# Cross-shaped window attention on one core: all matmuls in 64x64 tiles, VectorE's exponential as three shifted terms, and a written-out order

## The chip, the cores and the metric

The kernel runs on 1 core of a Trainium2 chip. The metric is the device time of one launch in microseconds. The kernel before takes 1006.58 us (median of 3 runs, 1004.67 to 1014.27).

## The reference

Input x is one image of 224 x 224 tokens with 96 channels in bf16. The channels are split in two halves of 48: the first half attends inside horizontal stripes of 8 rows, the second inside vertical stripes of 8 columns. There are 28 windows of each kind, and each has 1792 tokens.

```
qkv = einsum('bhwc,cd->bhwd', x, wqkv);  q, k, v = thirds of qkv
qh, kh, vh = first 48 channels, reshaped to (28, 8*224, 48)          # horizontal stripes
ah = softmax(qh @ kh^T * 48**-0.5);  oh = ah @ vh
qv, kv, vv = last 48 channels, transposed and reshaped to (28, 224*8, 48)   # vertical stripes
av = softmax(qv @ kv^T * 48**-0.5);  ov = av @ vv
out = concat(oh, ov) @ wo
```

The bulk is 56 windows of 1792 x 1792 scores, their exponentials, and the product of the exponentials with V.

## The kernel before, in words

Two windows are worked on together as a pair P (28 pairs: 14 horizontal, then 14 vertical), called w = 0 and w = 1; w = 0 lives on partitions 0 to 63, w = 1 on 64 to 127. The queries of a pair come in four chunks c of 512, 512, 512 and 256 (`CH`). The keys come in 14 tiles of 128. A *unit* is one key tile of a 512-chunk, or two key tiles of the 256-chunk, for both windows: 49 units per pair, 1372 in all.

For each unit TensorE computes the scores of both windows (`qk_op`, L1016: K^T of 48 rows x 128 keys against 512 queries) into two neighbouring PSUM banks. K is centred and scaled beforehand, Q carries the factor, and a unit's scores come out as 128 times the base-2 exponent. Then the unit's exponential is made in one of two ways:

- *ScalarE's units* (`add_a`, 1071 of them): one activation Exp over both banks into a tile PT (L1038). Then the values product (`pv_op`, L969: V of 128 keys x 64 columns against PT), one matmul per window into two column halves of the chunk's accumulator bank. A column of ones in V gives the sum of the exponentials.
- *VectorE's units* (`add_d`, 301 of them, `NDC` and `NDP` say how many per chunk, mostly two units together): VectorE adds an offset and converts to int16 (L1076, I_sb), whose bits read as bf16 are a rough power of two. Two mask steps (L1089, U_sb; L1091, E_sb) and a product I*U (L1095, G_sb; mostly on GpSimd in pieces of 512, else on VectorE) make a two-term correction: the values product is done twice, once with E and once with G.

When a chunk is complete VectorE evacuates the accumulator (L932, OT_sb); `fin` projects it with wo (L810, L844), takes the reciprocal of the sums (L797) and multiplies (L817, L854). Horizontal results are kept in Ph_sb; for vertical pairs GpSimd adds them (L860) and SyncE stores (L888, 16 stores per pair). Beside this `prep(P + 1)` projects K (L706), Q (L700) and V (L766) of the next pair with `fill` matmuls over all 96 channels (L686, L761); GpSimd centres K (L720). `load(P + 2)` brings x transposed, by DMA transposes on SyncE's queue (L558): one per horizontal window and eight per vertical one, into xT_sb, which has two buffers.

The order of all engines comes out of a `Planner` that runs when the kernel is built: per engine an order string (`PLAN["pe"]` and so on) names the stream that the next operation is taken from, a "bank" string the PSUM banks, and a "far" string which products go to GpSimd. Each engine's instructions then run strictly in that order, with semaphore waits for what they depend on. The chip's PSUM has eight banks; scores take two per unit, accumulators and fills one each.

The planner also keeps VectorE's fast SBUF-to-SBUF steps and GpSimd's operations apart (`lock`): a GpSimd operation waits for the last such VectorE step ahead of it.

Of the kernel before, what the change touches and what calls it, by code (L numbers as in the profile page):

```python
# [11 lines left out]
ALU = mybir.AluOpType  # L12

E_MID = 1.513  # L20
ONE = 127.0 - log2(E_MID)
M_FRAC, M_EXP, HALF, E_LOW = 0x007F, 0x7F80, 0x3F00, 0x0002


NDC = [4, 2, 2, 2]
NDP = {P: [3, 3, 3, 2] for P in range(28) if P % 4 != 1}


def ndc(P, c):
    return NDP.get(P, NDC)[c]  # L30


PLAN = {
    "pe": (
        "0000000000000000000000066611216162164144116444216331216431241641231431643441163446141541234133164412164412144312314"
        "31631451431244144126143153121433146124153341143444131235144123414414126413311463643164154134143163124614412614"
        "31145444134124163135164123135412144414412433112344144116344416312351431241641134445312416411463344144121543123"
        "14611364451231441163441233154113444412614412416312513411433444146123153114634413351541241634124136144123144116"
        "34434134124136134125144412316411463441213341146354154164144123133412314412414412316341163444135123164135414124"
        "41441461231634124133113644413312541441231641146344124313411634312441341261441231341441233144114644512316433153"  # L40
        "12416412314313411644431154444416415431531361241544123164114634114453341541231641241634125144144124133114434412"
        "54144113336412461441164431245143126134114533441414612351331241641146343124414411363412531441134464126134125144"
        "12413313412341541441163533416124415312461341144431163444412134412416313361441241541241631146441132331544113444"
        "12641441261331231341145444415412316311463433125144123164114534412341641146334144125413413312416441241641136441"
        "12444133113644312416441215431341241344123144164133123161331146345124153411444412361341134444615415416431313512"
        "44164123164114344412316311453441264134125144144124313312514414414611363354131254144123413416412416411463343141"
        "45124416313412416341241461113443344125144412133316412164412415411433334154124146134126133411634412441544121633"
        "11433544144164123154123146311446341241441164333125144113644512314314412441441612313412361341153444126133411263"
        "41441153444123416411463431333124154124163411264414411534441163354123164145123134412144414613312414312316441231"
        "44146135135312414414412613331163441144464451441331631241534124164114634114433441251344114644126314412514414123"  # L50
        "13412315411344436131641253144124163413514412416411463334143123146124134114644441214461133344125143411442154136"
        "12316412313313414412415441136446133125413124415411364441231544114634413313316441261341241641231441641144334125"
        "41341441231341241541241641146333134415413124414126133123154113644412315441146334154164144412613312316312464144"
        "11644341241334114634124415412415313613412413314364411444412531213314412313414313441241541163344143123154123154"
        "41146346114644611444463134151244415412316412416314412416411333441251344141153344412513341441241341241543164133"
        "14416412316312461441146443123144116336415312415314124413416412416412416412313313415441146341253134123154114464"
        "31244136144115343341431631241631241644126134114644412413311464441231334151244154124164124133113464431152344131"
        "34125134414412313415411463344154164164123163312416313464144126144144123153312414414412315312416411463331344164"
        "31441246144125144313412414414414615312361331231541136444412415411464441133644311344431531241531241641231641146"
        "44412413314441251334141125313341123444136144125144411463331463134125144412416411444334121641163363151244154124"  # L60
        "16312414316412164411433431231541144434415123315441231541144344123416411463341441246144121633113343412416441116"
        "36336124154124153124164134146124133124134134144415412415311633631541264431441254144134114334413441261331446121"
        "63414441231441126413311463441241541241531231614612431431331444144125143123314414412315441115336346113444641541"
        "64146163313613412414412614411344441231534124154124164114644412313412133411464441133633124415412315411344431251"
        "44411433441541241421316311366334166144164123134124144124154123153411466441313412441441231334154124153114444451"
        "312351331144444123313411434412541331241544113444124314311443152334154114421433114431433151534414445"),
    "dve": (
        "00000000000000000333333332332344323232443233313443432323244123443234323321342444133234423233333344133232333414"
        "23334323442322144313233244333233441323323333244312344323232344431323343133332342432344143232332344123443333332"
        "42421234413332344342333232144323323443214442323442424133321333244233344333331333233234431333323234243324124331"  # L70
        "32344323323344133323323444231323443323233244412334333132332443332144323233234431234432323244431333234312332344"
        "33233314423323234432144323423432412443123333244332344333333313323234412333234432321443233133323443232333413342"
        "32324431423443232324443134332312344323323344331323323443231233344234423321234431323234434323344132332323443313"
        "33234423442332124423133334423233443333132332344312333234421233244331332334432332334413232443231234432333234442"
        "41233431323323344323344413332323244314234423233234441344423132323344323344333313232323443214432332333444423144"
        "21244442343233441323323333334431333233234423231442313334234423233441343232334442133333423443232323444123343123"
        "32334443234441333323232344321444323323323214434441323234443233443331333234233442312344232332344344132314234442"
        "33332332334132334344441333233232344321444213323444323233443132332344432133333233244323234441233441332332344432"
        "34413232344432313332332334423324444412332313333323442344413423332444213234432332332334444421214423323333344333"
        "33333132234412332332344421234443132332344323441334232343333343242123323344334424412332313443432334442414423323"  # L80
        "34442144332343424444143333133333"),
    "pool": (
        "00000000022222221212122222222222222222112122222222222222221212122222222222222222221112222222222222222222211122"
        "22222222222222222121212222222222222222221212122222222222222222212112222222222222222222221212122222222222222222"
        "21212122222222222222222221112222222222222222222121212222222222222222222121212222222222222222222212121222222222"
        "22222222212121222222223223222232222121213222233332222322222121212222233322332232222333112122222222233223322331"
        "21213222232222332222121213222222333223222221211322222222333322222213131322223332222322222233321212123223222233"
        "2222222121212332232222223333221311222222332222222222212121232233332232222222222313112233322223333322333333"),
    "far": (
        "11111011110111111101111111111111111011111111110111011111111111111111101111111111111111111111111101111111111111"  # L90
        "11110111111111111111110111111111111111111111111110111011101100111111110010010111111010101101111001110111010111"
        "011110101100110110110111101101110111011100101101111111101011111011010100001000000"),
    "bank": (
# [23 lines left out]
class Op:  # L117
    __slots__ = ("eng", "occ", "lat", "fn", "deps", "soft", "alloc", "then", "wait", "tok", "dma", "mode", "start", "end", "lock", "segs", "kind", "far", "late")

    def __init__(s, eng, occ, lat, fn, deps=(), soft=(), alloc=(), then=None, dma=None, mode=None):  # L120
# [3 lines left out]
        s.kind, s.far, s.late = None, (), None  # L124


class Pool:


    def __init__(s, slots):  # L130
        s.slots = list(slots)
        s.free_by = {k: [] for k in s.slots}
# [1092 lines left out]
```

## Time and profile before

| what | value |
|---|---|
| median of 3 runs (range) | 1006.58 us (1004.67 to 1014.27) |
| profiled execution, span from first to last instruction | 1001.1 us (the page gives no other time of it) |
| PE (TensorE matmul) busy | 987.2 us, 99% |
| ACT (ScalarE) busy | 987.6 us, 99% |
| DVE (VectorE) busy | 938.3 us, 94% |
| POOL (GpSimd) busy | 684.3 us, 68% |
| granted TensorE clock | 0.998 |

How to read it: a busy PE is modelled, since matmuls are pipelined and overlap. In the rows of groups stand the line, the engine, the operation, output<-input with shapes and the count, then busy us and the mean ns of one, then the idle time of the engine just before and what ended it. In a timeline the first two numbers are start and length. PEld is the loading of weights for a matmul. The windows view gives, for each stretch, busy time and count on PE, PEld, DVE, ACT and POOL, the granted clock, and the DMA's share and GB/s.

### The profile page before, as it was taken

The numbers are of one execution on the slowest core, as the hardware profiler recorded it, in microseconds if no ns is written. First come the engines' busy times: TensorE is split into PE (matmuls) and PEld (weight loads), VectorE is DVE, ScalarE is ACT, GpSimd is POOL, SyncE is SP. The second block draws the span as 40 slices with busy tenths as digits, with TensorE's granted clock in tenths as the row PEclk, the third lists the DMA queues.
The fourth block names the chain that finished last, engine by engine and source line by source line (L and its number), as shares of the span: only waits on it lengthen the run. The fifth ranks groups of instructions, "written<-read, shape, count | busy, mean of one in ns | idle before, by whom it ended". The sixth has DMA issues, their size and how long they took to land.

```text
span 1001.1 us, 24570 instructions
## 1 busy us (share of the span) xinstructions
PE 987.2 (99%) x10216; PEld 385.3 (38%) x10216; DVE 938.3 (94%) x1573; ACT 987.6 (99%) x1080; POOL 684.3 (68%) x660
## 2 busy tenths in 40 slices
PE   8999999999999999999999999999999999999997
PEld 3333433343343334334334333433433443343342
DVE  8989999999999999999899999999999999999997
ACT  7999999999999999999999999999999999999997
POOL 3677776667677676777776776776676777677652
PEclk9999999999999999999999999999999999999999
DMA  5101110210222023011111122222122222222012
GB/s 110 39 7 33 38 38 2 38 39 1 38 39 32 7 38 38 2 37 24 26 30 32 26 46 49 54 50 46 36 40 53 52 52 41 52 52 37 16 34 52
DMA packets 164712, 36.92 MB, mean 37 GB/s; under 512 B 164488, under 2 KB 164488, under 8 KB 164600
## 3 DMA queue, kind: packets, MB, share of 16 engines
q1 hardware_dynamic: 163016, 34.80, 18.4%
q8 instruction: 80, 1.31, 0.5%
q10 hardware_dynamic: 1584, 0.55, 0.2%
q14 instruction: 32, 0.26, 0.1%
HBM read 0.44 MB, written 9.63 MB: 10 GB/s over the span
## 4 chain that ended last, share of the span: by engine, by line
ACT 70%; PE 28%; DVE 1%; DMA 0%; issue 0%
ACT PT L1038 70%; PE ps L969 13%; PE ps L1016 11%; PE ps L686 2%; PE ps L761 1%; PE ps L844 1%; DMA w_sb<-in_wqkv_dram 0%; PE ps L810 0%; DVE OT_sb L932 0%; DVE out_sb L867 0%; DVE I_sb L1076 0%; DVE U_sb L1089 0%; DVE E_sb L1091 0%; PE ps L679 0%; DVE KT_sb L706 0%
## 5 line engine op out<-in xcount | busy, mean ns | idle before, releaser
L1038 ACT ACTIVATE PT<-ps 128x1024 bf16<-128x1024 f32 x1071 | 983.5, 1114 | 2.9 <-PE ps L1016 1.5
L1095 POOL TENSOR_TENSOR G_sb<-I_sb,U_sb 128x512 bf16<-128x512 bf16 x482 | 544.1, 1153 | 250.0 <-DVE E_sb L1091 224.6
L1016 PE MATMUL ps<-QT_sb,KT_sb 48*128 48x512 bf16 (+1 forms) x3136 | 463.0, 356 | 4.7 <-ACT PT L1038 3.0
L1076 DVE TENSOR_SCALAR I_sb<-ps 128x1024 int16<-128x1024 f32 x301 | 367.4, 1220 | 24.7 <-PE ps L1016 21.3
L969 PE MATMUL ps<-PT,V_sb 128*64 128x512 bf16 (+1 forms) x2422 | 363.8, 363 | 1.1 <-ACT PT L1038 1.0
L1016 PEld LDWEIGHTS ps<-QT_sb,KT_sb 48*128 48x128 bf16 x3136 | 123.2, 93 | 307.4 <-ACT PT L1038 223.3
L969 PEld LDWEIGHTS ps<-PT,V_sb 128*64 128x64 bf16 x2422 | 119.2, 109 | 122.6 <-issue 94.9
L969 PE MATMUL ps<-G_sb,V_sb 128*64 128x512 bf16 (+1 forms) x714 | 115.7, 356 | 0.0
L969 PE MATMUL ps<-E_sb,V_sb 128*64 128x512 bf16 (+1 forms) x714 | 109.9, 356 | 0.5 <-DVE OT_sb L932 0.2
L1089 DVE TENSOR_SCALAR U_sb<-I_sb 128x2048 int16<-128x2048 int16 (+1 forms) x161 | 109.1, 678 | 0.2
L860 POOL TENSOR_TENSOR out_sb<-tmp,Ph_sb 128x480 bf16<-128x480 f32 (+1 forms) x84 | 84.9, 1025 | 30.0 <-DVE E_sb L1091 10.7
L1091 DVE TENSOR_SCALAR E_sb<-I_sb 128x2048 int16<-128x2048 int16 (+1 forms) x161 | 104.9, 652 | 0.2 <-PE ps L969 0.2
L686 PE MATMUL ps<-xT_sb,w_sb 96*64 96x512 bf16 (+1 forms) x444 | 77.5, 366 | 1.0 <-ACT PT L1038 0.5
L932 DVE CAST OT_sb<-ps 128x512 bf16<-128x512 f32 x112 | 69.3, 619 | 5.9 <-PE ps L969 5.0
L706 DVE TENSOR_SCALAR_CACHE_REDUCE KT_sb<-ps 128x512 bf16<-128x512 f32 x110 | 67.8, 620 | 7.4 <-PE ps L686 6.8
L700 DVE TENSOR_SCALAR QT_sb<-ps 128x512 bf16<-128x512 f32 (+1 forms) x111 | 68.1, 619 | 5.3 <-PE ps L686 4.1
L766 DVE CAST V_sb<-ps 128x480 bf16<-128x480 f32 (+2 forms) x85 | 51.7, 612 | 3.1 <-PE ps L761 2.8
L969 PEld LDWEIGHTS ps<-G_sb,V_sb 128*64 128x64 bf16 x714 | 36.4, 108 | 47.3 <-issue 28.8
L720 POOL TENSOR_SCALAR KT_sb<-KT_sb,negmean 128x1792 bf16<-128x1792 bf16 x27 | 47.5, 1759 | 10.3 <-DVE E_sb L1091 6.2
L817 DVE TENSOR_TENSOR Ph_sb<-ps,rc 128x480 bf16<-128x480 f32 (+1 forms) x84 | 52.3, 622 | 2.1
L854 DVE TENSOR_TENSOR tmp<-ps,rc 128x480 f32<-128x480 f32 (+1 forms) x84 | 51.9, 618 | 2.2
L969 PEld LDWEIGHTS ps<-E_sb,V_sb 128*64 128x64 bf16 x714 | 33.9, 108 | 42.9 <-issue 21.3
(49 smaller groups left out, 323.0 us busy)
## 6 DMA issues: line engine op xcount, KB each, us to landing
out_dram<-out_sb SPq DMA_DIRECT2D x208, 42.0 KB, 2.1
xT_sb<-in_x_dram SPq DMA_TRANSPOSE x251, 2.4
out_dram<-out_sb SPq DMA_DIRECT2D x22, 24.0 KB, 1.9
Ph_sb<-in_x_dram ACTq DMA_DIRECT2D x1, 336.0 KB, 3.1
out_dram<-out_sb ACTq DMA_DIRECT2D x6, 24.0 KB, 1.9
wo_sb<-in_wo_dram SPq DMA_DIRECT2D x4, 9.0 KB
wo_sb<-one_sb SPq DMA_DIRECT2D x4, 0.0 KB
w_sb<-in_wqkv_dram ACTq DMA_DIRECT2D x1, 54.0 KB, 4.7
```

Of the source, the lines that this page charges most:

```text
L686: ins = e.matmul(bk[64 * w:64 * w + 64, 0:qs], lhsT=w_sb[0:C, wblk(P, kind), :], rhs=rhs, start=True, stop=True)
L700: return e.tensor_scalar(dst, src, QS, None, ALU.mult)
L706: return e.tensor_scalar(dst, src, 1.0, None, ALU.mult, ALU.add, accum_out=acc)
L860: return e.tensor_tensor(out_sb[b][:, k0:k0 + nk, ws[0], :], t, Ph_sb[:, k0:k0 + nk, j0 + ws[0], :], ALU.add)
L932: return e.tensor_copy(OT_sb[b][:, q0:q0 + qs], bk[:, 0:qs])
L969: return e.matmul(bank(k.bank)[64 * w:64 * w + 64, x0:x1], lhsT=lhs(w, kts[i])[p0:p1], rhs=rhs(w, i, qs)[p0:p1, x0:x1], start=(op.tok["fir ...
L1016: ins = e.matmul(bank(op.tok["s"][w])[:, i * qs:(i + 1) * qs], lhsT=KT_sb[b][64 * w:64 * w + C2, kt * 128:(kt + 1) * 128], rhs=QT_sb[b][64 ...
L1038: a.fn = lambda e: e.activation(PT[a.tok["p"]][:].rearrange("p (s n) -> p s n", s=2), two(q.tok["s"]), ACTF.Exp, scale=LN128)
L1076: return e.tensor_scalar(dst[:, at:at + 1024].rearrange("p (s n) -> p s n", s=2), two(src), 128.0 * ONE, 0.0, ALU.add, ALU.max)
L1089: f.fn = lambda e: e.tensor_scalar(U_sb[y()][:, 0:m], I_sb[y()][:, 0:m], M_FRAC, HALF, ALU.bitwise_and, ALU.bitwise_or)
L1091: x2.fn = lambda e: e.tensor_scalar(E_sb[x2.tok["l"]][:, 0:m], I_sb[y()][:, 0:m], M_EXP, E_LOW, ALU.bitwise_and, ALU.bitwise_or)
L1095: g.fn = lambda e: e.tensor_tensor(G_sb[x2.tok["l"]][:, i0:i1], I_sb[y()][:, i0:i1].bitcast(BF16), U_sb[y()][:, i0:i1].bitcast(BF16), ALU. ...
```

## The change

- *Tiles.* Every matmul of the steady state uses 64x64 tiles of the array. Scores of window w go from row half w to column half w, in two half-units of 64 keys (`qk`); each half-unit's two windows share one bank, on different partition halves. Values go from row half w to column half 1 - w (`pv`), with 64 keys at a time and V of 50 columns. K, Q and V projections are done in two halves of 48 channels on the scores' tiles; the output projection uses 49 rows. PE has four semaphores instead of one, by tiles used.
- *Layout of x.* So that half the channels of both windows stand on the two partition halves, window 0 is transposed into xa_sb and window 1 into a staging tile xr_sb; three SBUF-to-SBUF copies per pair (SyncE's queue) place the rest. wqkv is loaded a second time in halves (w2_sb).
- *VectorE's units.* 13 per pair instead of 10 or 11 (`ND`), so 364; ScalarE has 1008. For 11 of the 13, the exponential is the sum of three bf16 readings: of I, of I + 43 and of I + 85, with V scaled by 2^(-43/128) and 2^(-85/128) for the last two (Vs_sb, made by GpSimd once per pair). The adds are int16 steps over one or two units, 272 on GpSimd and 64 on VectorE; the values product is done three times. Two units per pair keep the old masks and product.
- *Order.* The planner is gone. One string `SEQ` (10743 letters) gives the order of everything, and `BANK` the banks; each engine runs its own operations in that order.

The core of the diff (the old strings and the planner's classes, which go, are left out):

```diff
-NDC = [4, 2, 2, 2]
-NDP = {P: [3, 3, 3, 2] for P in range(28) if P % 4 != 1}
+T_MID = 3.122
+ONE3 = 127.0 - log2(T_MID)
+SHIFT = (43, 85)
+ND = ["4432"]
+QUAD = [(5,)]
...
+    S, M = 0.2165, 0.0315
...
 def load(P, stream):
...
+                dst_, sem_ = (xr_sb, s_xr) if w else (xa_sb[b], s_x[b])
...
+                if not w:
+                    hi = wk.add(stream, Op("sp", 0.65, lambda e: e.dma_start(xb_sb[b][0:C2, 0, :], xa_sb[b][C2:C, 0, :]), [op] + war, ...))
+            for src, dst in ((0, xa_sb), (C2, xb_sb)):
+                last = wk.add(stream, Op("sp", 0.65, lambda e, src=src, dst=dst: e.dma_start(dst[b][64:64 + C2, 0, :], xr_sb[src:src + C2, 0, :]), [op, hi], ...))
...
 K and Q projections:
+                    for i in range(1 if startup else 2):
+                        for w in range(2):
+                                src, wt = (xa_sb, xb_sb)[i][b][64 * w:64 * w + C2, 0, :], w2_sb[i][64 * w:64 * w + C2, wblk(P, kind), :]
+                            ins = e.matmul(out_, lhsT=wt, rhs=rhs, start=i == 0, stop=startup or i == 1)
...
+        def qk(u, stream):
+            for h, t in enumerate(ts):
+                th = [2 * kts[0] + h] if len(kts) == 1 else [2 * kts[h], 2 * kts[h] + 1]
+                def fn(e, t=t, th=th):
+                    for i, k in enumerate(th):
+                        for w in range(2):
+                            ins = e.matmul(bank(t.k)[64 * w:64 * w + 64, i * qs:(i + 1) * qs], lhsT=KT_sb[b][64 * w:64 * w + C2, 64 * k:64 * k + 64],
+                                           rhs=QT_sb[b][64 * w:64 * w + C2, q0:q0 + qs], start=True, stop=True)
...
+        def pv(u, stream, ts, rhs, deps, vk=None):
+            for h in range(2):
+                        for w in range(2):
+                            ins = e.matmul(bank(k_.slot.k)[64 - 64 * w:64 - 64 * w + CP, 0:qs], lhsT=V_[64 * w:64 * w + 64, k, :],
+                                           rhs=rhs()[64 * w:64 * w + 64, h * 512 + i * qs:h * 512 + (i + 1) * qs], ...)
...
+        def add_d(units, quad):
+            if quad:   # the old masks and products
...
+            else:
+                for dst, c, war in ((U_sb[y], SHIFT[0], []), (E_sb[l], SHIFT[1], l_war)):
+                    fn = lambda e, dst=dst, c=c: e.tensor_scalar(dst[:, 0:m], I_sb[y][:, 0:m], float(c), 1.0, ALU.add, ALU.mult)
+                    us.append(wk.add("U", Op("pool", 0.23 + 0.83 * m / 1000, fn, ds + war, alt=fn)))
+                terms = [("d", I_sb[y], ..., None), ("d", U_sb[y], ..., 0), ("D", E_sb[l], ..., 1)]
...
+        wk.run(SEQ, BANK)
```

More of the change, by code (lines that the diff above doesn't have):

```diff
@@ L465, in bass_standalone__window_attn_cswin__vision_kernel @@
-        live = []
-        class Home:
-            def __init__(s, digits, each):
-                s.digits, s.each = digits, each
-            def peek(s, when, n):
-                at = pl.bank + pl.ahead
-                ks = [int(d) + i for d in PLAN["bank"][at:at + s.digits] for i in range(s.each)]
-                got = dict((k, t) for t, k in banks.order(when))
-                if any(k not in got for k in ks):
-                    return None
-                return (max(got[k] for k in ks), ks)
-            def take(s, ks):
-                pl.bank += s.digits
-                deps = []
-                for i in range(0, len(ks), s.each):
-                    deps += banks.take(ks[i:i + s.each])
-                return deps
-            def free(s, k, by):
-                for i in k if isinstance(k, list) else [k]:
-                    banks.free(i, by)
@@ new lines, in fin, with store @@
+                    held_rc.append(ops[1:2])
+                    if not last:
+                        held_tmp.append(ops[2:3])
+                    fin_pe[P] = [p]
+                    def store(eng, k, w, by):
+                        dst = bass.AP(out.tensor, out.offset + (16 * k * W + SW * (j0 + w)) * C, [[W * C, 16], [1, SW * C]])
+                        out_dma[P].append(wk.add("Z" if eng == "act" else "y", Op(eng, 0.64, lambda e: e.dma_start(dst, out_sb[b][:, k, w, :]), by, lat=2.0, dma=s_out[b])))
@@ new lines, in fin @@
+                    added[P].append(ops[-1])
+                    if last:
+                        for s in range(n):
+                            store("act" if s % 2 else "sp", k0 + s % nk, ws[s // nk], [ops[1 + s]])
+                    elif P == NP - 1:
+                        side = "act" if c == NCH - 2 and ws[0] else "sp"
+                        for k in range(k0, k1):
+                            for w in ws:
+                                store(side, k, w, ops[-1:])
+                    elif len(added[P]) == 2 * (len(VB) - 1):
+                        for d in range(SW):
+                            for w in range(2):
+                                dst = bass.AP(out.tensor, out.offset + (SW * (j0 + w) + d) * C, [[W * C, 16], [16 * W * C, NKT], [1, C]])
+                                fn = lambda e, dst=dst, d=d, w=w: e.dma_start(dst, out_sb[b][d:128:SW, :, w, :])
+                                out_dma[P].append(wk.add("y", Op("sp", 0.64, fn, added[P], lat=2.0, dma=s_out[b])))
@@ L1024, in add_a @@
+            last_qk[P][stream] = ops[1]
+            return ops, ts
+        def pv(u, stream, ts, rhs, deps, vk=None):
             P, c, kts = u
             b = P % 2
[L1026 to L1036 removed]
@@ new lines, in pv, with fn @@
+            q0, qs = CH[c]
+            k_ = chunks[(P, c)]
+            ops = []
+            for h in range(2):
+                vs = [o for i0, i1, o in v_ready[P] if any(i0 <= 2 * k + d < i1 for k in kts for d in range(2))] if vk is None else [vs_ready[P][vk]]
+                V_ = V_sb[b] if vk is None else Vs_sb[b][vk]
+                def fn(e, h=h, n=len(k_.ops), V_=V_):
+                    me = k_.ops[n]
+                    hh = h if ts[0].k < ts[1].k else 1 - h
+                    th = [2 * kts[0] + hh] if len(kts) == 1 else [2 * kts[hh], 2 * kts[hh] + 1]
+                    for i, k in enumerate(th):
+                        for w in range(2):
+                            ins = e.matmul(bank(k_.slot.k)[64 - 64 * w:64 - 64 * w + CP, 0:qs], lhsT=V_[64 * w:64 * w + 64, k, :],
+                                           rhs=rhs()[64 * w:64 * w + 64, h * 512 + i * qs:h * 512 + (i + 1) * qs],
+                                           start=me is k_.first and i == 0, stop=me is k_.end and i == len(th) - 1)
+                    return ins
+                o = wk.add(stream, Op("pe", S, fn, [deps[h]] + vs, take=[k_.slot], mode="v"))
+                k_.ops.append(o)
+                ops.append(o)
@@ L1146, in bass_standalone__window_attn_cswin__vision_kernel @@
             if P + 2 < NP:
[L1147 removed]
+                load(P + 2, "X")
             if P + 1 < NP:
[L1149 to L1172 removed]
+                prep(P + 1)
```

1194 lines of the change are left out of this document (436 added, 758 removed).

## The prediction

> **What bounds the kernel now.** I read the page's busy shares first, then the chain that ended last, then a table of stages, then the waits.
>
> ```profile
> PE 987.2 (99%) x10216; PEld 385.3 (38%) x10216; DVE 938.3 (94%) x1573; ACT 987.6 (99%) x1080; POOL 684.3 (68%) x660
> ...
> ACT 70%; PE 28%; DVE 1%; DMA 0%; issue 0%
> ...
> L1038 ACT ACTIVATE PT<-ps 128x1024 bf16<-128x1024 f32 x1071 | 983.5, 1114 | 2.9 <-PE ps L1016 1.5
> ```
>
> ```profile
> 300.00:500.00 200.00, 199.11 (x2158) 76.47 (x2154) 183.47 (x303) 200.00 (x220) 143.48 (x135) 1.00 0.16 25
> ...
> 700.00:900.00 200.00, 198.72 (x2008) 78.70 (x2006) 192.98 (x318) 199.06 (x217) 138.86 (x134) 1.00 0.24 47
> ```
>
> ```profile
> PEld ps L1016 <- ACT PT L1038: 223.3, 694, 0.8
> ```
>
> Two engines read 99%, but they are not alike. ScalarE (ACT) is really full: in the stages it is busy 200.00 and 199.06 of 200 us, its 1071 exponentials take 983.5 us (0.918 us each, start to start), and it idled 2.9 us before them. TensorE's 99% is modelled; its weight loads waited 223.3 us, in 694 pieces, for an exponential to free a bank. So ScalarE sets the pace, TensorE is close behind it, and VectorE (94%) is third. The granted clock is 1.00.
>
> The ends of the chain, which the change hardly touches:
>
> ```profile
> 7.45 0.81 PE L761 MATMUL ps<-w_sb,xT_sb 96*64 96x48 bf16 x40
> ...
> 9.07 3.77 ACT L1038 ACTIVATE PT<-ps 128x1024 bf16<-128x1024 f32 x4 [0.71 <-PE ps L1016]
> ...
> 994.87 0.41 PE L969 MATMUL ps<-PT,V_sb 128*64 128x256 bf16 x4 [0.51 <-ACT PT L1038]
> 994.91 2.80 ACTq L888 DMA_DIRECT2D out_dram<-out_sb  x4
> ```
>
> Exponentials run from 9.07 to 994.9; the last 6.2 us of the 1001.1 us span are the last evacuation, projection and store.
>
> **ScalarE.** The change gives it 1008 exponentials of the same shape instead of 1071: 63 x 0.918 = 58 us less. Alone it would need 9.07 + 1008 x 0.918 + 6.2 = 941 us. That is the gain on offer; the rest of the change has to pay for the 63 units that move to VectorE.
>
> **TensorE.** Today scores use two tiles of 64 rows x 128 columns, values two of 128 x 64. A run of equal pairs, and a change between kinds, read so:
>
> ```profile
> 506.42 0.38 PE L969 MATMUL ps<-G_sb,V_sb 128*64 128x512 bf16 x2
> 506.73 0.39 PE L1016 MATMUL ps<-QT_sb,KT_sb 48*128 48x512 bf16 x2
> 507.05 0.62 PE L969 MATMUL ps<-PT,V_sb 128*64 128x512 bf16 x4
> ...
> 520.48 1.03 PE L969 MATMUL ps<-PT,V_sb 128*64 128x512 bf16 x8
> ```
>
> Four pairs last 1.03 us and one pair 0.39, so a pair costs (1.03 - 0.39) / 3 = 0.213 us: its two matmuls run side by side. A change of kind costs 0.31 and 0.32 instead of 0.213, so 0.10 us more. The order string of before changes kind 1783 times: some 178 us of TensorE. With every tile 64x64 these should go, and that is the second thing the change removes.
>
> In return each unit takes two score pairs (row tile w to column tile w, the diagonal) instead of one, and two value pairs (the other two tiles) per term. Counting: diagonal 1372 units x 2 = 2744 pairs; off the diagonal 1008 x 2 for ScalarE's units, 308 x 6 for VectorE's three-term units and 56 x 4 for its two-term ones, 4088 pairs. I price a pair at 0.2165 us (the figure in the diff, 1.5% above the row's 0.213; the row is the low end). Diagonal: 594 us, plus K, Q and V projections, now in two halves of the contraction on the same tiles: 27 pairs of windows x (14 x 0.2165 + 56 x 0.0315) = 129 us, the 0.0315 from the 40 small matmuls above (20 pairs in 0.81 us, less the 0.19 us that one lasts). Sum 723. Off the diagonal: 885, plus the output projection, 28 x 28 blocks at the diff's 0.046 and 0.05 us, 38, half of which takes all tiles. Sum 923. No row of before shows four tiles at once. Lower end: diagonal and other tiles overlap fully, and the time is the larger sum. Upper end: never more than one pair at once, 723 + 923 = about 1646 us. I take the lower end, since the rows show row tiles side by side (L1016) and column tiles side by side (L969) each without loss. Walking the new order, where a step starts when the step before it has started and its own tiles are free, gives 928 us: the order loses only 5. From 7.4, where the first projections start, with the 6.2 us tail: 7.4 + 928 + 6.2 = 942 us. So ScalarE (941) and TensorE (942) end together, each with 1 to 2% to spare.
>
> On the score pair, its two matmuls come from different row tiles and write the same bank, on different partition halves; before, they wrote two banks. The Trainium skill, "TensorEngine Tiling (Array Packing)", section "Gotcha 1: PSUM Pressure", says that different row tiles cannot access one bank at the same time; "PSUM — Partial Sum Buffer", section "PSUM bank collisions raise a hardware error", narrows the measured fault to one bank and the same 32-partition quadrant, which these halves do not share. By the first the sum would be the upper end, by the second the lower; no run here shows either. The first is a rival below.
>
> **VectorE.** Rows:
>
> ```profile
> L1076 DVE TENSOR_SCALAR I_sb<-ps 128x1024 int16<-128x1024 f32 x301 | 367.4, 1220 | 24.7 <-PE ps L1016 21.3
> ...
> L1089 DVE TENSOR_SCALAR U_sb<-I_sb 128x2048 int16<-128x2048 int16 x140 | 99.9, 713 | 0.1
> L1091 DVE TENSOR_SCALAR E_sb<-I_sb 128x2048 int16<-128x2048 int16 x140 | 96.1, 686 | 0.2 <-PE ps L969 0.2
> ...
> L1095 DVE TENSOR_TENSOR G_sb<-I_sb,U_sb 128x1024 bf16<-128x1024 bf16 x60 | 41.9, 707 | 0.1
> ...
> L1089 DVE TENSOR_SCALAR U_sb<-I_sb 128x1024 int16<-128x1024 int16 x21 | 9.2, 440 | 0.0
> L1091 DVE TENSOR_SCALAR E_sb<-I_sb 128x1024 int16<-128x1024 int16 x21 | 8.8, 419 | 0.0
> ```
>
> Added: 63 more conversions (77 us). Removed: the mask pairs, with the smaller form 99.9 + 9.2 + 96.1 + 8.8 = 214 us, fall to 28 of each (39 us), and products fall from 60 to 31 (20 us less). New: 64 shifted adds on int16, 41 of 2048 and 23 of 1024; like the masks at 0.70 and 0.42 they cost 38 us, at the conversion's rate (2.4 and 1.2) 126. I take 38, the same shape and dtypes. Net about -80: 858 of some 950 us, 90%; at the upper price 946, full. Evacuations stay.
>
> **GpSimd (POOL).** Rows:
>
> ```profile
> L720 POOL TENSOR_SCALAR KT_sb<-KT_sb,negmean 128x1792 bf16<-128x1792 bf16 x27 | 47.5, 1759 | 10.3 <-DVE E_sb L1091 6.2
> L860 POOL TENSOR_TENSOR out_sb<-tmp,Ph_sb 128x480 bf16<-128x480 f32 (+1 forms) x84 | 84.9, 1025 | 30.0 <-DVE E_sb L1091 10.7
> L1095 POOL TENSOR_TENSOR G_sb<-I_sb,U_sb 128x512 bf16<-128x512 bf16 x482 | 544.1, 1153 | 250.0 <-DVE E_sb L1091 224.6
> ```
>
> 432 of 482 products go (50 x 1.153 = 58 us stay); 272 shifted adds come, 523,264 elements per partition in all. No int16 form runs on GpSimd before. Nearest row: L720, one input, 1759 / 1792 = 0.98 ns per element; far row: L1095, two inputs, 2.25 ns. I take 0.98, one input: 514 us. Two scaled copies of V per pair add 56 x 1400 x 0.98 = 77, L860 86, the K steps 58 (47.5, and two tiny sums for each). Sum 793. The 250 us of idle before L1095 shows that GpSimd is held while VectorE does its masks; of those, adds and products about 100 us are left on VectorE. 893 of 934 us: it fits, with little to spare. At r ns per element GpSimd needs 379 + 523 r; it sets the end from r = 1.06.
>
> **SyncE and the loads.** x for a second window now goes through a staging tile with three SBUF copies, so SyncE issues 16 transposes, 3 copies and 16 stores per vertical pair of windows, and waits for landings in between. Rows:
>
> ```profile
> 604.51 11.14 SPq L888 DMA_DIRECT2D out_dram<-out_sb  x16
> 615.69 14.10 SPq L558 DMA_TRANSPOSE xT_sb<-in_x_dram  x11
> 629.83 11.06 SPq L888 DMA_DIRECT2D out_dram<-out_sb  x16
> ...
> xT_sb<-in_x_dram SPq DMA_TRANSPOSE x251, 2.4
> ```
>
> A transpose takes 14.14 / 11 = 1.29 us of the queue, a store 11.18 / 16 = 0.70. Per pair 16 x 1.29 + 19 x 0.70 = 33.9 us against 36 x 0.918 = 33.0 of exponentials. Over the last 12 pairs that is 11 us late; the order has 13 exponentials (12 us) between a load's last copy and its first use at pair 14, but only 3 (2.8 us) from pair 20 on, about one landing (2.4). What is late next is the first K projection of the next pair; TensorE is in order, so all of scores and values wait behind it. The stores are put into the landing waits. I take 4 us; ends 0, and 50 if both landings (2 x 2.4) stay open in 12 pairs, less the 12 us of lead.
>
> **Other edits.** A unit holds its two banks some 0.2 us longer, and two engines at 98% leave each other's jitter uncovered: 6 us, between 0 and 14 (before, the same coupling cost ScalarE 2.9). The weight copies for projections go behind the first loads on SyncE; eight exponentials pass before the first use, so nothing.
>
> **Sum.** 942 + 4 + 6 = 952 us of span. The span before is 1001.1 and the runs' median 1006.58, 5.5 more; the page gives nothing else around the span. So **957 us**.
>
> **Rivals.**
> - *SyncE sets the pace of the second half* (landings not covered). For it: 33.9 against 33.0, before any wait. Against: stores lie in the gaps. Time 957 + half to all of 46: 980 to 1003; I say 985.
> - *GpSimd becomes the bound, slower.* The int16 adds cost more than 0.98 ns. Decides from 1.06; from r = 1.2 (379 + 628 = 1007, plus ends) the kernel is slower. At L1095's 2.25 it is 379 + 1177 = 1556, about 1575. For: unseen form, VectorE's port in the way. Against: one input, as L720.
> - *The change doesn't do what it says:* tiles of the two kinds do not overlap, because of the shared bank or of the order. 7.4 + 1646 + 6.2 + 5.5 = 1665 us. For: no row shows four tiles. Against: both pairings run without loss.
>
> **How the numbers follow.** Forecast 0.71, SyncE 0.11, GpSimd 0.09, tiles 0.09. Own range of the forecast: 944 (ScalarE's 941 and 3.6 us around it, the lowest run's 1004.67 less the span) to 975. The whole range goes up to 1000 for SyncE and a mild GpSimd; the two slow cases stay out. Runs of this kernel spread over 1%, so 1% (10 us) is what a measurement can tell. Faster: 0.71 + 0.09 of SyncE = 0.80; within 1%: 0.02 of SyncE and 0.01 of a mild GpSimd = 0.03; slower: 0.08 of GpSimd + 0.09 = 0.17.
>
> **What would show it.** Right: ACT still above 97%, 1008 exponentials at 0.918; score and value matmuls starting within a pair's time of each other; no wait of 0.10 between kinds; shifted adds on POOL near 2.0 us for 2048; POOL near 85%. Wrong: ACT below 95% with PE waiting at the K projection for a DMA (SyncE); value matmuls waiting for U_sb or E_sb from POOL (GpSimd); pairs in single file (tiles).

## The result, and the profile after

The changed kernel takes 1022.95 us (median of 4 runs, 1018.27 to 1024.78) against 1005.62 us for the kernel before: ratio 1.015, 95% interval 1.0103 to 1.0197. It is 1.5% slower, where 957 us was forecast; 1023 also lies outside the range of 944 to 1000. The profiled run took 1021.68 us with a span of 1019.9.

The page of the profile after: the busy shares, and the chain that ended last, by engine.

```profile
PE 982.9 (96%) x21130; PEld 667.7 (65%) x21130; DVE 884.5 (87%) x1405; ACT 947.1 (93%) x1017; POOL 766.3 (75%) x554
...
PE 75%; SPq 14%; DMA 4%; POOL 2%; DVE 2%; issue 1%; ACT 1%; POOLq 0%; ACTq 0%
```

Before, the chain was 70% ScalarE (ACT) and no queue stood in it. Now ScalarE is 93% busy and 1% of the chain, TensorE (PE) is 75%, and SyncE's queue (SPq) with its landings 18%. Two things are to be explained: TensorE where ScalarE was expected, and SyncE.

The windows view in stages of 99 us (columns: stage, its length, then busy time and count for PE, PEld, DVE, ACT, POOL; last three the granted clock, DMA share, GB/s):

```profile
119.00:218.00 99.00, 98.97 (x2186) 68.76 (x2180) 89.49 (x139) 97.26 (x105) 78.74 (x54) 1.00 0.26 43
...
416.00:515.00 99.00, 99.00 (x2206) 68.62 (x2205) 88.44 (x140) 97.11 (x105) 79.49 (x54) 1.00 0.22 47
...
614.00:713.00 99.00, 90.68 (x2017) 64.74 (x2011) 81.50 (x127) 86.32 (x93) 71.78 (x53) 0.95 0.28 57
713.00:812.00 99.00, 93.59 (x1980) 63.64 (x1974) 83.65 (x133) 88.16 (x94) 77.38 (x57) 0.97 0.28 58
812.00:911.00 99.00, 90.41 (x1934) 58.60 (x1930) 82.19 (x131) 87.41 (x95) 69.73 (x54) 0.97 0.29 60
```

There are two losses. Up to about 640 us a stage holds 105 or 106 exponentials (101 in the stage from 20 us), about 0.943 us each, not 0.918, with TensorE full. After that it holds 93 to 95, and TensorE itself is idle for 5 to 9 us per stage.

What TensorE waits for in the second case, from the waits of the kernel after (total us, times, longest):

```profile
PE ps L522 <- DMA xb_sb<-xr_sb: 25.1, 7, 8.0
...
ACT PT L787 <- PE ps L748: 49.7, 71, 9.1
```

L522 is the K and Q projection. Seven times it waits up to 8.0 us for the last copy of x, and ScalarE then waits up to 9.1 us for scores. The queue that issues the copy, over one vertical pair of windows (from 639.23 to the next pair's first transpose at 678.50):

```profile
639.23 10.66 SPq L411 DMA_TRANSPOSE xa_sb<-in_x_dram  x8
652.77 0.58 SPq L415 DMA_DIRECT2D xb_sb<-xa_sb  x1
653.39 12.40 SPq L411 DMA_TRANSPOSE xr_sb<-in_x_dram  x8
665.84 3.19 SPq L732 DMA_DIRECT2D out_dram<-out_sb  x5
669.13 0.58 SPq L417 DMA_DIRECT2D xa_sb<-xr_sb  x1
669.75 0.59 SPq L417 DMA_DIRECT2D xb_sb<-xr_sb  x1
670.38 8.07 SPq L732 DMA_DIRECT2D out_dram<-out_sb  x11
678.50 12.01 SPq L411 DMA_TRANSPOSE xa_sb<-in_x_dram  x8
```

The issues add up to 36.1 us, and from 649.89 to 652.77 the queue waits for the first window to land. The pair takes 39.3 us (the eight pairs from 596.89 to 907.73 take 38.9 in the mean); its 36 exponentials need 33. So SyncE sets the pace there.

And the loss where SyncE is idle. TensorE's timeline in the kernel after around one V projection (L602), cut to its ends; L771 are the value matmuls, L748 the scores:

```profile
132.44 0.38 PE L771 MATMUL ps<-I_sb,V_sb 64*50 64x512 bf16 x2
132.56 0.38 PE L748 MATMUL ps<-QT_sb,KT_sb 48*64 48x512 bf16 x2
132.66 0.38 PE L771 MATMUL ps<-I_sb,V_sb 64*50 64x512 bf16 x2
132.78 0.19 PE L602 MATMUL ps<-w_sb,xa_sb 48*64 48x48 bf16 x2
132.81 0.19 PE L602 MATMUL ps<-w_sb,xb_sb 48*64 48x48 bf16 x2
...
133.28 0.19 PE L602 MATMUL ps<-w_sb,xa_sb 48*64 48x48 bf16 x2
133.29 0.40 PE L771 MATMUL ps<-PT,V_sb 64*50 64x512 bf16 x2
...
133.41 0.38 PE L748 MATMUL ps<-QT_sb,KT_sb 48*64 48x512 bf16 x2
133.53 0.38 PE L771 MATMUL ps<-PT,V_sb 64*50 64x512 bf16 x2
```

Normally the two kinds run beside each other, a pair of each per 0.22 us (132.44 and 132.66; 132.56 and, but for the projection, 132.78). But from 132.66 to 133.29 no value pair starts. In between 17 pairs of the V projection are issued, one per 0.0315 us. They use the score tiles only. At the pace of one value pair per 0.22 us the value tiles are empty from 132.88 on and stay so for 0.41 us, because the next value pair stands behind the projection in TensorE's program. The Trainium skill, "TensorE: Matmul & The Clock Gate", section "Step-by-step: what each phase is for", says that matmuls stay in program order and only weight loads are pulled ahead. These rows agree but for three pairs: the value pair waits for 17 of the projection's 20 pairs, and by the starts that the profile gives it goes ahead of the last three, which come up to 133.38.

### The profile page after: what moved, and what is told of

Its sections match the earlier page's. It is cut to its first block, busy times and chain, and to the rows that moved or that the text cites. A ratio compares the mean times of both kernels' runs of the same rounds, so it can differ in the third digit from the quotient of the medians.

```text
span 1019.9 us, 47123 instructions
## 1 busy us (share of the span) xinstructions
PE 982.9 (96%) x21130; PEld 667.7 (65%) x21130; DVE 884.5 (87%) x1405; ACT 947.1 (93%) x1017; POOL 766.3 (75%) x554
## 4 chain that ended last, share of the span: by engine, by line
PE 75%; SPq 14%; DMA 4%; POOL 2%; DVE 2%; issue 1%; ACT 1%; POOLq 0%; ACTq 0%
PE ps L771 39%; PE ps L748 26%; SPq L411 9%; SPq L732 4%; PE ps L522 4%; PE ps L602 4%; DMA xb_sb<-xr_sb 3%; PE ps L656 1%; DVE I_sb L805 1%; POOL out_sb L696 1%; PE ps L686 1%; POOL U_sb L821 1%; ACT PT L787 1%; SPq L415 1%; DMA xa_sb<-in_x_dram 1%
## 5 line engine op out<-in xcount | busy, mean ns | idle before, releaser
L748 PE MATMUL ps<-QT_sb,KT_sb 48*64 48x512 bf16 (+1 forms) x6272 | 765.0, 359 | 0.5 <-ACT PT L787 0.2
L771 PE MATMUL ps<-PT,V_sb 64*50 64x512 bf16 (+1 forms) x4592 | 532.6, 353 | 0.0
L748 PEld LDWEIGHTS ps<-QT_sb,KT_sb 48*64 48x64 bf16 x6272 | 274.5, 106 | 152.7 <-ACT PT L787 58.7
L821 POOL TENSOR_SCALAR U_sb<-I_sb 128x2048 int16<-128x2048 int16 (+1 forms) x137 | 245.7, 1794 | 58.5 <-DVE I_sb L805 37.3
L771 PEld LDWEIGHTS ps<-PT,V_sb 64*50 64x50 bf16 x4592 | 241.9, 101 | 48.3
L821 POOL TENSOR_SCALAR E_sb<-I_sb 128x2048 int16<-128x2048 int16 (+1 forms) x135 | 242.8, 1799 | 34.8 <-DVE U_sb L821 13.4
L771 PE MATMUL ps<-U_sb,Vs_sb 64*50 64x512 bf16 (+1 forms) x1344 | 196.9, 362 | 0.0
L771 PE MATMUL ps<-I_sb,V_sb 64*50 64x512 bf16 (+1 forms) x1344 | 191.6, 361 | 0.5 <-DVE tmp L690 0.2
L771 PE MATMUL ps<-E_sb,Vs_sb 64*50 64x512 bf16 (+1 forms) x1344 | 178.1, 364 | 0.0
L522 PE MATMUL ps<-xa_sb,w_sb 48*64 48x512 bf16 (+3 forms) x440 | 79.1, 359 | 26.6 <-DMA xb_sb<-xr_sb 25.1
L814 POOL TENSOR_TENSOR G_sb<-I_sb,U_sb 128x512 bf16<-128x512 bf16 x50 | 57.1, 1157 | 53.3 <-DVE E_sb L810 31.0
L771 PEld LDWEIGHTS ps<-E_sb,Vs_sb 64*50 64x50 bf16 x1344 | 72.8, 102 | 18.2
L771 PEld LDWEIGHTS ps<-U_sb,Vs_sb 64*50 64x50 bf16 x1344 | 72.7, 101 | 17.9
L771 PEld LDWEIGHTS ps<-I_sb,V_sb 64*50 64x50 bf16 x1344 | 67.8, 100 | 18.5 <-ACT PT L787 1.3
L522 PE MATMUL ps<-xb_sb,w_sb 48*64 48x512 bf16 (+2 forms) x436 | 77.3, 355 | 0.0
```

The lines of the kernel that those rows point to most:

```text
L522: ins = e.matmul(out_, lhsT=wt, rhs=rhs, start=i == 0, stop=startup or i == 1)
L748: ins = e.matmul(bank(t.k)[64 * w:64 * w + 64, i * qs:(i + 1) * qs], lhsT=KT_sb[b][64 * w:64 * w + C2, 64 * k:64 * k + 64], rhs=QT_sb[b][6 ...
L771: ins = e.matmul(bank(k_.slot.k)[64 - 64 * w:64 - 64 * w + CP, 0:qs], lhsT=V_[64 * w:64 * w + 64, k, :], rhs=rhs()[64 * w:64 * w + 64, h * ...
L821: fn = lambda e, dst=dst, c=c: e.tensor_scalar(dst[:, 0:m], I_sb[y][:, 0:m], float(c), 1.0, ALU.add, ALU.mult)
```

## Experiments

Two theories were tested one after the other. A: SyncE's queue sets the pace of the second half. V: the in-order issue of V projections holds the value tiles empty. Rivals were landing latency (C), and work that the engines themselves do (B; in the first runs that of VectorE and GpSimd in the second half, later ScalarE and TensorE losing time to each other over banks everywhere). Experiments 1 to 4, 5 to 8 and 9 to 11 were each made on one chip, where the kernel before took 1006.21, 1005.47 and 1004.60 us; a difference in us between two groups is good to about 2 us.

**1. Nearly no stores.** 15 of the 16 stores per vertical pair are left out.

```diff
-                        for d in range(SW):
-                            for w in range(2):
+                        for d in (SW - 1,):
+                            for w in (1,):
```

> Of the 16 stores that SyncE issues for a vertical pair of windows only the last is left, for 13 pairs (most of the output is not written). Theory A (SyncE's queue is the pace of the second half: some 36.7 us of issues and 3 us of waits per pair, against about 33.4 us that the engines need): the queue falls to about 28 us per pair, no K projection waits for a copy, the TensorE clock stays at 1.00, and the time is 950 to 962 us. Theory B (the vertical half is slower by its own work on VectorE, GpSimd or in the banks, and SyncE is late with it): 1000 us or more. Theory C (landing waits alone, not issues): the waits stay, 990 to 1015.

Measured: 985.26 us (ratio to before 0.9765, 0.9736 to 0.9793). The waits of L522's line for a copy are gone, and the late stages are like the early ones:

```profile
713.00:812.00 99.00, 99.00 (x2193) 72.41 (x2190) 91.47 (x143) 96.03 (x104) 80.79 (x60) 1.00 0.21 44
812.00:911.00 99.00, 98.98 (x2200) 66.35 (x2192) 91.97 (x146) 96.74 (x105) 80.74 (x61) 1.00 0.20 41
```

A holds for 38 us of the miss. But 950 to 962 was expected: the pace stops at 0.943 us per exponential, with TensorE full. A second loss was left.

**2. No copies.** The second window is transposed straight to its place, and the three copies go (so K, Q and V are not the reference's).

```diff
-                dst_, sem_ = (xr_sb, s_xr) if w else (xa_sb[b], s_x[b])
+                dst_, sem_ = (xb_sb[b], s_xc[b]) if w else (xa_sb[b], s_x[b])
...
-                    hi = wk.add(stream, Op("sp", 0.65, ...))
-                last = wk.add(stream, Op("sp", 0.65, ...))
```

> The staging tile and its three copies per pair go: window 1 is transposed straight into the second tile, and the projections run on the same tiles with what then stands there (K, Q and V are not the reference's). Theory A: the queue needs 16 transposes and 16 stores, about 35 us per pair and no landing wait, 1.5 us over the engines' 33.4 for ten pairs, mostly covered by the lead: 955 to 970 us. Theory B: 1000 or more. If the copies' traffic made the transposes dearer (1.45 us each now, 1.29 to 1.38 before), they come back to 1.36 or less and the time is at the low end.

Measured: 991.3 us (0.982, 0.9782 to 0.9858). That is 21 us above A's range. Three short issues with their landings are worth 32 us, nearly as much as 15 stores, since with 15 stores less the gain ended at TensorE's own limit. Here the queue takes 36.7 us per pair (589.91 to 883.62, eight pairs), and the late stages hold 103 to 105 exponentials. The transposes take 1.47 us each, so the traffic of the copies is not what makes them dear.

**3. The first copy issued later**, halfway through the second window's transposes, so that the queue need not wait for the landing.

```diff
                 for i, (tr, dst, s_) in enumerate(todo):
+                    if w and i == len(todo) // 2:
+                        hi = wk.add(stream, Op("sp", 0.65, lambda e: e.dma_start(xb_sb[b][0:C2, 0, :], xa_sb[b][C2:C, 0, :]), [low] + war, ...))
```

> Order on SyncE alone: the copy out of the first window's tile is issued halfway through the second window's eight transposes, not before them, so its landing wait is gone. Theory A: 1 to 2 us less per pair, 1000 to 1012 us. Theory C (landing waits are the main part): 970 to 990. Theory B: no change, 1018 to 1025.

Measured: 1014.22 us (1.0071, 1.0044 to 1.0099), 9 us less than the change. That is nearest to A, 2 us beyond its range; C's 970 to 990 is refuted. A pair takes 38.0 us instead of 38.9. The landing wait is a small part, the sum of the issues the large one: in the changed kernel the copies wait for a landing three times from 600 to 970 us, 6.7 us in all, and the pair shown above has the longest of these waits.

**4. Six of 16 stores issued by ScalarE.** All work stays.

```diff
-  ... Op("sp", 0.64, fn, added[P], lat=2.0, dma=s_out[b])
+  ... Op("act" if 2 * d + w in (0, 3, 6, 9, 12, 15) else "sp", 0.64, fn, added[P], lat=2.0, dma=s_out[b])
```

> 6 of the 16 stores of a vertical pair are issued by ScalarE, at the same places of the order. Theory A: SyncE falls by 6 x 0.73 = 4.4 us per pair to about 35.3, ScalarE rises by 6 x 0.62 = 3.7 to 36.8 us per pair and sets the pace of some eleven pairs: 980 to 995 us. Theory B: ScalarE's added work comes on top, 1030 or more.

Measured: 987.64 us (0.9787, 0.975 to 0.9824), in A's range, and faster than both kernels. A's reason was another, though, and the number is luck: ScalarE was to set the pace by the price of its stores, but the late stages hold 104 or 105 exponentials as in experiment 1, with TensorE full. The stores' data still moves here (62 to 64 GB/s in these stages, 57 to 60 in the changed kernel), so it is the issuing on SyncE that cost time, not the traffic. The next three build on this kernel.

**5. Half of the V projection.**

```diff
-                        for i in range(1 if startup else 2):
+                        for i in range(1):
```

> On top of the kernel with six stores per vertical pair issued by ScalarE (987.6 us, 0.943 us per exponential in every stage), each V projection sums only the first half of its channels: 28 row pairs of 48 columns per pair of windows instead of 56; the values are not the reference's. Theory V (the in-order issue of a V projection's 16 to 20 small pairs, one per 0.0315 us, holds back the value matmuls on the other two tiles; the trace shows their tiles idle 0.2 to 0.4 us there): 28 x 0.0315 = 0.88 us less issue per pair of windows, of which 0.85 us is idle time of the value tiles, 27 times, about 22 us: 962 to 970. Theory B (TensorE and ScalarE lose the 3% to each other over the score banks, everywhere): the removed work lies on the score tiles, which have 100 us to spare, so 983 to 988.

Measured: 967.62 us (0.9615, 0.9596 to 0.9634). 20 us go, as V says, although the work taken away lies on the tiles that have time to spare. B is refuted as the main cause.

**6. V projections in pieces.** All work stays; after each piece of 8 row pairs comes one value pair of the order.

```diff
+                cut = [0, n] if startup else [*range(0, n, 4), n]
+                parts = [lambda e, bk, j0=j0, j1=j1: pe_fn(e, bk, j0, j1) for j0, j1 in zip(cut[:-1], cut[1:])]
...
+            if op.rest:
+                queued = list(op.rest)
+            elif queued and q in "cdD":
+                r = queued.pop(0)
+                s.place(r, r.deps)
```

> On the same kernel, each V projection is cut into pieces of 8 row pairs (0.25 us), and one value pair of the order goes between two pieces; all the work stays. Theory V: the value tiles idle about 0.04 us per piece instead of up to 0.4 per step, so some 20 us of the 28 come back: 962 to 972. Theory B: 985 to 990.

Measured: 969.57 us (0.9634, 0.9612 to 0.9657). TensorE's timeline around a V projection, here L617, with the values at L788:

```profile
130.49 0.38 PE L788 MATMUL ps<-I_sb,V_sb 64*50 64x512 bf16 x2
130.60 0.19 PE L617 MATMUL ps<-w_sb,xa_sb 48*64 48x48 bf16 x2
...
130.74 0.40 PE L788 MATMUL ps<-PT,V_sb 64*50 64x512 bf16 x2
...
130.99 0.40 PE L788 MATMUL ps<-PT,V_sb 64*50 64x512 bf16 x2
...
131.22 0.38 PE L788 MATMUL ps<-PT,V_sb 64*50 64x512 bf16 x2
```

Value pairs now start every 0.23 to 0.25 us through the projection. In the early stages ScalarE is at its own pace, 107 to 108 exponentials. Late ones fall to 104; there the K projection (L537) waits for a copy again, 6.4 us in all after 640 us:

```profile
218.00:317.00 99.00, 98.93 (x2233) 66.24 (x2230) 90.69 (x142) 98.89 (x108) 81.94 (x56) 1.00 0.27 50
...
713.00:812.00 99.00, 97.28 (x2127) 64.86 (x2120) 91.79 (x145) 96.02 (x104) 79.50 (x59) 1.00 0.32 66
```

**7. Half as much exponential.**

```diff
-  e.activation(split(PT[i % NPT]), two(ts), ACTF.Exp, scale=LN128)
+  e.activation(split(PT[i % NPT])[:, :, 0:m], two(ts)[:, :, 0:m], ACTF.Exp, scale=LN128)   # m = 256 after the first 8
```

> On the same kernel without the split, ScalarE's exponentials after the first eight take half the columns (the other half of their tile keeps old values, so the output is not the reference's). ScalarE is then about half idle and frees banks early. Theory V: TensorE's order alone sets the pace, 975 to 987. Theory B: without ScalarE at its limit the coupling goes and TensorE runs at its tile sum of 923 to 928 us plus the ends, 940 to 950.

Measured: 979.61 us (0.9731, 0.9713 to 0.9749). ScalarE is 62% busy, a stage still holds 104 to 106 (102 in the stage from 20 us), and TensorE is full:

```profile
119.00:218.00 99.00, 99.00 (x2206) 71.59 (x2198) 89.78 (x140) 61.62 (x106) 79.07 (x55) 1.00 0.24 42
```

So TensorE's order sets the 0.943. The 8 us that do go are at most what coupling with ScalarE had in it.

**8. Pieces alone**, on the changed kernel with SyncE as it was (the edit of 6 without that of 4).

> The changed kernel with only the V projections cut as above; SyncE's queue is as in the changed kernel. Theory V with SyncE (each sets its own part): the first half, where SyncE has few instructions, gains about 13 us, the second half still goes at SyncE's 39.7 us per vertical pair: 1005 to 1014. If SyncE alone set everything: 1018 to 1025. If V were the whole loss: 990 or less.

Measured: 1007.18 us (1.0006, 0.9988 to 1.0025), 16 us below the change and level with the kernel before. The early stages hold 107 or 108, the late ones 93 to 96 as in the change: each cause sets its own half.

**9. Both causes away** (the edits of 1 and 6).

> Both causes away together: the V projections cut in pieces, and 15 of the 16 stores of each of 13 vertical pairs left out (that part of the output is not written). If the two causes are the whole miss, the prediction's own sum is what is left: ScalarE at 0.921 us per exponential as in the first stages of the cut kernel, 9 + 1008 x 0.921 + 6 + 2 = 945, and some us of coupling: 950 to 962, with 107 exponentials in every 99-us stage. If a third cause sits in the second half (VectorE and GpSimd do more evacuations there), 965 to 972, with the late stages at 104.

Measured: 965.57 us (0.9598, 0.9561 to 0.9636), every stage after the first at 106 to 108. It is 3.6 us over the first expectation's range, and the second has the time but not the stages (104 late): what is left is not one late stage but a little everywhere (below).

**10. All work kept, eight stores on ScalarE, late copy, pieces** (edits 3, 4 and 6, with the odd stores on ScalarE).

> All work stays: V projections in pieces, 8 of 16 stores per vertical pair issued by ScalarE, and the copy of the first window's second half issued halfway through the second window's transposes. SyncE per vertical pair: 16 x 1.45 + 3 x 0.62 + 8 x 0.73 = 30.9 us against 36 x 0.921 = 33.2: SyncE no longer sets the pace, 955 to 965, against 969.6 with 10 stores on SyncE and the copy early. If ScalarE pays for its stores with its own time (about 0.56 us each on its queue, 104 of them), 975 to 1010.

Measured: 968.16 us (0.9629, 0.9582 to 0.9676). Its stages are those of 9, so SyncE is off the path:

```profile
713.00:812.00 99.00, 98.98 (x2157) 68.89 (x2152) 93.55 (x148) 97.83 (x106) 79.37 (x59) 1.00 0.32 66
```

With 6 it is the best version that does all the work: 3.7% less than before. The intervals of the two overlap, so the late copy and two more stores cannot be told from nothing.

**11. Ten stores on ScalarE.**

> As the one before, with 10 of 16 stores on ScalarE: SyncE 29.5 us per vertical pair. Same time within 3 us of it if SyncE is off the path already; 3 to 8 us less if its queue still decides.

Measured: 971.66 us (0.9661, 0.9623 to 0.9699), 3.5 us over experiment 10, where the same time or less was expected. ScalarE's timeline shows the price of its stores:

```profile
785.77 1.09 ACT L806 ACTIVATE PT<-ps 128x1024 bf16<-128x1024 f32 x1
786.38 1.59 ACTq L751 DMA_DIRECT2D out_dram<-out_sb  x1
788.08 1.02 ACT L806 ACTIVATE PT<-ps 128x1024 bf16<-128x1024 f32 x1 [1.21 <-PE ps L790]
788.18 0.79 ACTq L751 DMA_DIRECT2D out_dram<-out_sb  x1
```

An issue of 0.56 us hides behind the exponential that runs; one that takes 1.59 us does not, and the next exponential starts 2.31 us after the last. The row puts the wait down to a value matmul, but the issue ends at 787.97, 0.11 us before the exponential starts. The same gap of 0.09 to 0.11 us stands behind nine long issues of this run (0.85 to 1.59 us, whatever matmul is named), with 4.0 us of idle time before the nine exponentials; experiment 10 has two such places with 0.5 us. The difference, 3.5 us, agrees with that of the two times. Why some issues take so long was not tried.

## Why the prediction was wrong, step by step

- **ScalarE, 941 us: right as a price.** 108 exponentials in a 99-us stage of experiment 6 are 0.917 us each. (983.5 / 1071 = 0.918 is busy time; from start to start the exponentials before took 0.920, 2 us more over all of them.) It was not the bound.
- **TensorE's tiles: right.** Score and value pairs run side by side at 0.215 to 0.22 us (0.24 for the first behind a pause), with no 0.10 us between kinds, and the shared bank costs nothing that the rows show. The Trainium skill's rule of one bank for one row tile ("TensorEngine Tiling (Array Packing)", "Gotcha 1: PSUM Pressure") does not show itself for these partition halves; the narrower rule of the Trainium skill's "PSUM — Partial Sum Buffer", "PSUM bank collisions raise a hardware error", agrees with the rows. The rival of 1665 us is refuted.
- **TensorE's walk, 928 us: the first step that failed.** The walk let a step start "when the step before it has started". A V projection is one step of 16 or 20 row pairs, and what stands behind it has to wait until almost all of them are issued. By the prediction's own 0.0315 us (the row that it cites gives 0.62 / 20 = 0.031, the rows after 0.0315), steps of 20, 20 and 16 pairs hold the queue for 0.60, 0.60 and 0.47 us; less the 0.2165 us that a value pair lasts, the value tiles stay empty for 0.38, 0.38 and 0.26, 1.02 us per pair of windows and an estimated 28 us in 27 of them. 942 becomes 970, and ScalarE and TensorE no longer end together. The traces bear it out: the longest stretch between two value pairs at each V projection, less 0.2165, adds up to 25.4 us in the kernel after, 3.5 in experiment 5 and 3.8 in experiment 6. Experiment 5 gave back 20 us of time, experiment 6 18. Nothing new had to be known for this; the unit of the walk was wrong.
- **SyncE, 4 us: the second step that failed**, and the larger. "A transpose takes 14.14 / 11 = 1.29 us" was the cheapest row of before; others of the same queue read

```profile
762.74 15.98 SPq L558 DMA_TRANSPOSE xT_sb<-in_x_dram  x12
...
817.87 27.04 SPq L558 DMA_TRANSPOSE xT_sb<-in_x_dram  x20
```

  that is 1.33 and 1.35, and the mean of all 251 is 1.36. In the kernel after, over the eight pairs from 596.89 to 907.73, a transpose takes 1.46 (2.7 us more per pair than counted) and a store 0.74 instead of 0.70 (0.6 more). And "the stores are put into the landing waits" did not make the waits nothing: 1.7 us per pair are left, 2.88 at once in the pair shown. 33.9 us became 38.9; over twelve pairs that is 60 us more than was counted, of which the lead of the order and TensorE's slower pace took up a part. With the mean of before the sum would have been 35.1, still too little; why a transpose takes 1.46 in the kernel after stays open. The rival "SyncE sets the pace of the second half" named the mechanism and its place, the K projection waiting for a copy, but its 980 to 1003 was made with the same 1.29.
- **VectorE, 858 us: 884.5.** The instructions' own times fell by 81 us, about as counted (80). But neighbours overlap (before, they add up to 1032.7 us in 938.3 of busy time), and so the busy time fell by 54 only. GpSimd, 793: 766. An add of 2048 took 1.90 us, 0.93 ns per element where 0.98 was taken; neither became the bound.
- **Coupling, 6 us: some 21.** Experiment 9 has a span of 963.8 where the sum without SyncE's 4 says 948. The exponentials start at 9.93 instead of 9.07, then

```profile
13.93 1.02 ACT L818 ACTIVATE PT<-ps 128x1024 bf16<-128x1024 f32 x1 [0.23 <-PE ps L779]
15.95 3.77 ACT L818 ACTIVATE PT<-ps 128x1024 bf16<-128x1024 f32 x4 [1.00 <-PE ps L779]
21.55 8.78 ACT L818 ACTIVATE PT<-ps 128x1024 bf16<-128x1024 f32 x9 [1.83 <-PE ps L779]
...
924.71 31.43 ACT L818 ACTIVATE PT<-ps 128x1024 bf16<-128x1024 f32 x34
```

  and end at 956.1, not at 9.07 + 1008 x 0.918 = 934.4. Of these 21.7 us, 4.2 are lost by the tenth exponential (21.55 instead of 17.3), for want of scores; the rest is spread over all stages, about 2 us in those with 106 instead of 108. The tail is 7.7 us instead of 6.2. What the spread part consists of no run separates.
- **Around the span, 5.5 us: 1.8** (1021.68 less 1019.9). The 5.5 was the median of the runs less the span of one execution, and so mostly the spread between executions.

Together: experiment 1 takes 37.7 us off the change, experiment 8 15.8, and both 57.4 (experiment 9), of the 66 us between 1022.95 and the forecast. So the two steps are the bulk of the miss.

## What to carry to other kernels

An in-order engine with several independent tiles is not the larger of its tile sums: count, for each tile, the time in which the queue is busy issuing for another, and cut long runs of short instructions into pieces no longer than one instruction of the other tile. A queue that is planned at 100% of the pace must be priced with the mean of its rows, not the cheapest, with the waits that stand in order between them, and with a margin: here even the mean of before fell 3.8 us per pair short. When the first relief brings back only part of a miss and the rest is spread evenly over all stages, look for a second cause before refining the first.

## What the runs showed of the hardware

- Halves of one bank, written by two row tiles at once, ran without loss: 0.215 us per pair, where the rows before gave 0.213 for two banks.
- The granted clock falls in a stall of the second half: the stage from 647 to 680 us of the kernel after, with one wait of 8.0 us in it, has 0.84.

```profile
614.00:647.00 33.00, 32.80 (x744) 22.73 (x737) 30.44 (x50) 32.28 (x35) 27.79 (x21) 1.00 0.27 55
647.00:680.00 33.00, 24.95 (x544) 17.97 (x540) 20.73 (x31) 22.16 (x25) 19.12 (x13) 0.84 0.28 58
```

  In shorter windows the clock is 1.00 up to 667 us, where TensorE has been idle for 2 us, 0.52 from 667 to 671, 0.50 to 675, 0.76 to 680 and 1.00 from there. TensorE starts again at 673.0, and matmuls of the K projection then take up to 0.63 us instead of 0.38. So a late copy costs more than its wait: an estimated 2 us here, half of the 4 us or so that TensorE works at 0.50. Over the whole run no experiment separates it.
- ScalarE issues a store in 0.56 us beside a running exponential at no cost that the runs show. Single issues take longer, up to 1.47 us with eight stores per pair and 1.59 with ten, and those push an exponential back: 0.5 us in all with eight, 4.0 with ten.
- Matmuls on different tiles do not start strictly in the order of the program: in 61 of the 81 V projections of the kernel after, the value pair that comes behind the projection starts ahead of its last two or three short pairs, by up to 0.09 us.
